# Gated linear attention with a tanh-shrink feed-forward: the state update's products moved behind the output products, into the same PSUM bank

## The chip, the cores and the metric

The kernel runs on one core of one Trainium2 chip. A time is the device time of one execution in microseconds (us). The kernel before was run five times; its time is the median of those. One further execution was recorded by the hardware profiler, and all views below come from it. The engines are named as in the profile: PE is TensorE (matmul), PEld its weight load, DVE is VectorE, ACT is ScalarE, POOL is GpSimd, SP is SyncE, which here only issues transfers.

## The reference

For each of 4 batches and 8 heads, a 48x48 state is decayed and updated at each of 768 positions, and read by q. The result, as rows of 384 features, goes through a feed-forward with h - tanh(h) in the middle.

```python
def _attn_ref(q, k, v, alpha):
    for t in range(S):
        state = alpha[:, :, t, :, None] * state + np.einsum('bhd,bhe->bhde', k[:, :, t], v[:, :, t])
        y[:, :, t] = np.einsum('bhd,bhde->bhe', q[:, :, t], state)

def _moe_ref(x, w_in, w_out):      # x: 3072 x 384, w_in: 384 x 2048, w_out: 2048 x 384
    h = x @ w_in
    return (h - np.tanh(h)) @ w_out
```

## The kernel before

**Units and chunks.** The 3072 rows are worked in 12 units of 256 positions of one batch, three units to a batch. A unit has two chunks of 128 positions. In each chunk the recurrence is written as matrix products: cumulative products of alpha (two scans on VectorE per unit) scale k and q, and then, per chunk:

- `scores` (L757): k times q, 8 matmuls into two PSUM banks, sc0 and sc1.
- `masked` (L767): VectorE multiplies the scores by a triangular mask into SBUF.
- `products` (L780 to L809), task name `y`: the old state times q (L795) and v times the masked scores (L807), 16 matmuls into two PSUM banks. They reuse the banks of the scores. Head pairs g = 0 and 2 go to the first bank, g = 1 and 3 to the second, each to 128 columns, so that half of each bank's 512 columns stays free.
- `features` (L811), task name `x`: ScalarE copies y to SBUF as xT, one copy for each bank (L820).
- `back` (L822): k is transposed on TensorE (L825), into the first bank. `natural` (L827): ScalarE copies it to SBUF as kn (L829).
- `update` (L831): k times v, 8 matmuls (L836), into a tile that takes the second bank anew.
- `state` (L839): VectorE adds it to the decayed state (L844). ScalarE does it for a batch's first chunk (L842).

The last chunk of a batch has no back, natural, update and state. That leaves 20 updates. Unit 0 (`direct` in the code) takes other banks and has its own rules; 18 updates belong to units 1 to 11. An fp32 matmul shows as two MATMUL records in the trace, so an update is x16 there.

**Shapes on the array.** L944, L989, L1004 and L825 use 128 output columns. L807 and L836 use all 128 rows of the array but 48 or 64 columns, in two halves side by side; L795 uses 64 x 64 parts, L757 64 rows by 128 columns.

**The feed-forward.** Each unit has 8 steps. `first` (L944) multiplies xT by two column blocks of w_in. ScalarE and VectorE turn h into g (Square L953, quadratic L957, L961, L965) and for units from 2 on also into sums e (L977 to L979). `second` multiplies g, or the sums, by w_out: L989 for units 0 and 1, L1004 after that.

**The weights.** w_in and w_out arrive as 64-bit numbers in 8 pieces each, called in0 to in7 and out0 to out7 below. A piece is fetched (L43, by SP), read twice by ScalarE (L83, L84) and finished by VectorE (L86, L87). Steps 0 to 7 of unit 0 use them as they come. From unit 2 on, five precombined copies of w_out (`combine`) are needed.

**The order.** A planner (`Planner`, L319) gets every task with an engine, an assumed duration, a rank and the tasks it follows. It plays them through in eight rounds and writes out one fixed order for each engine. The engines then run their queues in order, with waits on semaphores that the framework adds. An assumed duration costs nothing in itself, but changes the order of every engine. In the order before, `update` must follow `x`:

```python
                    go_c("natural", "ACT", 0.6, 6.5, ["back", past and not past_last and f"update {past}"], natural)
                    go_c("update", "PE", 0.5, 9.5, ["natural", f"load v {u}", u > 0 and "x"], update)
```

At the end, a verdict on the ranges of the data (`judge` on VectorE, `gather` on TensorE, L1097) decides whether a general version has to run; here it doesn't.

Of the kernel before, what the change touches and what calls it, by code (L numbers as in the profile page):

```python
# [17 lines left out]
P = 128  # L18
HP = 64
CU = 2  # L20
# [298 lines left out]
class Planner:  # L319
# [13 lines left out]
    def add(self, name, engine, us, rank, after, do, lat=0.25):  # L333
        kind = name.rsplit(" ", 1)[0]
        self.tasks.append((name, engine, us, rank, [a for a in after if a], do, lat, self.last.get(kind)))
        self.last[kind] = name
# [85 lines left out]
def fast(tc, q, k, v, alpha, moe_w_in, moe_w_out, out, w_in, w_out, ident, ok, pad_rows):  # L422
    nc = tc.nc
    B, H, S, D = q.shape
    NP = H // 2
# [10 lines left out]
    V, A, T, GP = nc.vector, nc.scalar, nc.tensor, nc.gpsimd  # L436
# [3 lines left out]
    with ExitStack() as ctx:  # L440
# [84 lines left out]
        ROWS = HP + D  # L525

        def head(g, r):

            return 2 * g + (r + g) % 2
# [17 lines left out]
        for n, (what, s) in enumerate(pieces):  # L549
            rank = RANK[what] + 2 * s  # L550
            held = pieces[n - 4] if n >= 4 else None
# [38 lines left out]
        def gla(u, rank):  # L590
# [5 lines left out]
            m = {}  # L596

            direct = u == 0
# [112 lines left out]
            def done(by, what):  # L711

                return lambda u: [f"{by}{ab} {u}" for ab in "ab"] if by_matmul(u, what) else [f"{by} {u}"]
            kU, qW = done("kU", 1), done("qW", 2)
# [12 lines left out]
            def bank(n, c):  # L727


                if u < PLAIN:  # L730
                    return ps_o.tile([P, NP, P], FP32, name="y", tag=f"o{n if c is None else 2 + n}")
                return ps_sc.tile([P, NP, P], FP32, name="y", tag=f"sc{n}")

            def chunk(c):
                n = i * CU + c
                last = n == NCH - 1
                old, new = states[n % 2], states[(n + 1) % 2]
                me = f"{u}.{c}"
                past = f"{u}.{c - 1}" if c else f"{u - 1}.{CU - 1}" if u else None
                past_last = n == 0  # L740

                def go_c(name, engine, us, k, after, do, **kw):
                    add(f"{name} {me}", engine, us, rank + 6 * c + k,
                        [a if a[-1] in "0123456789" else f"{a} {me}" for a in after if a], do, **kw)
# [35 lines left out]
                def products():  # L780
# [23 lines left out]
                    for g, r, hh in pairs:  # L804
# [3 lines left out]
                                 rhs=m["pm", c][r][:, g, :],  # L808
                                 start=(n == 0 and g < (1 if direct else 2)), stop=True, skip_group_check=True)  # L809

                def features():  # L811
                    to = slice(c * P, (c + 1) * P)
                    y = m["y", c]
                    if n == 0 and direct:
                        A.copy(xT[u][:, 0:KT, to], y[0][:, 0:KT, :])
                        return
                    for x in range(2):
                        of = range(x, KT if direct else NP, 2)
                        rows = P if direct else ROWS
                        A.copy(xT[u][0:rows, of.start:of[-1] + 1:2, to], y[x][0:rows, 0:len(of), :])  # L820
# [8 lines left out]
                    A.copy(kn[:, :, 0:ROWS], m["tp", c][:, :, 0:ROWS])  # L829

                def update():  # L831
                    up = m["up", c] = bank(1, c)
                    for g in range(NP):
                        for r in range(2):
                            size = D if r else HP
                            T.matmul(up[HP * r:HP * r + size, g, 0:D], lhsT=m["kn", c][:, g, HP * r:HP * r + size],  # L836
                                     rhs=vts[u][:, c, head(g, r), :], start=(g == 0), stop=True, skip_group_check=True)

                def state():  # L839
                    up = m["up", c][0:ROWS, :, 0:D]  # L840
                    if n == 0:
                        A.copy(new[0:ROWS, :, 0:D], up)  # L842
                    else:
                        V.tensor_add(new[0:ROWS, :, 0:D], old[0:ROWS, :, 0:D], up)  # L844

                held = []
                if past and not (u == 0 and c == 1):
                    held = [f"masked {past}"]
                    if u > PLAIN or u == PLAIN and c:
                        held += [f"x {past}", not past_last and f"state {past}", not last and "natural"]  # L850
                go_c("scores", "PE", 1.05, 7, kU(u) + qW(u) + held, scores)
                go_c("masked", "DVE", 1.4, 8, ["scores", f"y 0.0" if u == 1 and c == 0 else past and u > 0 and f"y {past}"], masked)
                if n > 0:
                    go_c("decay", "DVE", 0.4, 6, [f"ends {u}", f"state {past}"], decay)
                if direct:
                    go_c("gaps", "ACT", 0.7, 7, [f"load v {u}", n > 0 and "decay", n > 1 and f"y {past}"], gaps)
                go_c("y", "PE", (1.9 if n == 0 else 3.4) if direct else 0.95 if n == 0 else 1.45, 9,
                     ["masked", f"load v {u}", n > 0 and "decay", direct and "gaps",
                      u > 0 and f"x {past}", u > 0 and not past_last and f"state {past}", u > 0 and not last and "natural"], products)
                go_c("x", "ACT", 0.6 if direct and n == 0 else 0.75, 10, ["y"], features)  # L860
                if not last:
                    go_c("back", "PE", 0.5, 6, kU(u) + [past and not past_last and f"state {past}", u > 0 and c and f"x {past}",
                                                       u > PLAIN and f"x {past}", u == PLAIN and not c and f"masked {past}"], back)
                    go_c("natural", "ACT", 0.6, 6.5, ["back", past and not past_last and f"update {past}"], natural)
                    go_c("update", "PE", 0.5, 9.5, ["natural", f"load v {u}", u > 0 and "x"], update)
                    go_c("state", "DVE" if n else "ACT", 0.4, 10,
                         ["update", n > 0 and "decay",
                          n > 0 and not past_last and f"y {past}"], state)

            for c in range(CU):  # L870
                chunk(c)
# [300 lines left out]
```

## Time and profile before

| | |
|---|---|
| median of 5 runs | 601.17 us (601.00 to 602.72) |
| profiled execution | 605.04 us |
| its span, first to last instruction | 603.3 us |
| TensorE's mean granted clock | 0.993 |
| update L836, TensorE | x320 records, 208 / 222 / 257 ns (min / median / max) |
| state L844, VectorE | x16, 354 ns median |
| xT L820, ScalarE | x46, 373 ns median |

Duration columns count a matmul from its start to its modelled end, and such records overlap. What a group takes from TensorE is therefore read from the start of its first matmul to the start of the next group's. A line of the timeline is: start in us, length in us, engine, line of the code, operation, output and inputs, sizes, number of records; in brackets the idle time of the engine ahead of it and what ended that.

### The profile page before, as it was taken

To read this page: it belongs to the slowest core of one execution; us is meant where nothing else is said; L and a number is where in the kernel's file an instruction comes from. 1 tells how busy PE (TensorE), PEld (TensorE's weight loads), DVE (VectorE), ACT (ScalarE), POOL (GpSimd) and SP (SyncE) were. 2 spreads that over 40 slices of the span, in tenths; PEclk is the share of its full clock that TensorE was granted. 3 is DMA by queue.
4 is the path that set the end of the run, shared out by engine and by line. 5 is a ranking of instruction groups with operands and counts; after the bars stand their busy time and mean duration, and the time that the engine had idled before them with its cause. 6 is when DMAs were issued, how large, how long until landed. Compare 5 with 4: busy or idle time off the path is not lost.

```text
span 603.3 us, 10673 instructions
## 1 busy us (share of the span) xinstructions
PE 587.0 (97%) x4113; PEld 508.8 (84%) x4113; DVE 437.6 (73%) x830; ACT 325.6 (54%) x585; POOL 4.0 (1%) x18
## 2 busy tenths in 40 slices
PE   8988999999999999999999999999999999999994
PEld 8766777768998898998898898898898898899994
DVE  7874897988796887986776796885797555634642
ACT  2677896636577575776566264364443333423430
POOL 2000000000000000000000000000000000000000
PEclk9998999999999999999999999999999999999998
DMA  9999962133675544562260131220010000000001
GB/s 182 188 225 228 269 140 59 54 85 79 110 144 123 120 133 116 121 153 75 79 170 27 36 77 28 56 81 3 29 32 1 30 4 1 27 9 1 26 1 33
DMA packets 60188, 50.63 MB, mean 84 GB/s; under 512 B 35264, under 2 KB 49888, under 8 KB 60128
## 3 DMA queue, kind: packets, MB, share of 16 engines
q1 hardware_dynamic: 57216, 48.88, 35.1%
q10 hardware_dynamic: 2912, 0.98, 0.8%
q8 instruction: 34, 0.56, 0.4%
q14 instruction: 26, 0.21, 0.1%
HBM read 44.04 MB, written 4.72 MB: 81 GB/s over the span
## 4 chain that ended last, share of the span: by engine, by line
PE 89%; DMA 7%; SPq 1%; ACT 1%; ACTq 0%; issue 0%; DVE 0%; DVEq 0%
PE h L944 41%; PE o L1004 31%; PE o L989 6%; PE sc L757 4%; PE y L807 4%; DMA raw<-in_moe_w_in_dram 2%; PE y L795 2%; DMA raw<-in_moe_w_out_dram 2%; PE y L836 2%; DMA vt<-in_v_dram 2%; PE y L825 1%; DMA rough<-in_q_dram 1%; SPq L43 1%; DMA ar<-in_alpha_dram 1%; ACTq L581 0%
## 5 line engine op out<-in xcount | busy, mean ns | idle before, releaser
L944 PE MATMUL h<-xT,w_in 128*128 128x256 f32 x1152 | 268.7, 383 | 1.3 <-DVE w_in L87 1.3
L944 PEld LDWEIGHTS h<-xT,w_in 128*128 128x128 f32 x1152 | 215.2, 191 | 31.6 <-DVE w_in L87 1.9
L953 ACT ACTIVATE u<-h 128x512 f32<-128x512 f32 x96 | 57.1, 595 | 181.3 <-PE h L944 180.7
L961 DVE TENSOR_TENSOR w<-h,u 128x512 f32<-128x512 f32 x96 | 65.9, 686 | 91.5 <-ACT u L953 91.4
L1004 PE MATMUL o<-b,e 128*128 128x192 f32 x480 | 91.1, 326 | 0.0
L1004 PE MATMUL o<-w_out,e 128*128 128x192 f32 x320 | 81.2, 335 | 0.0
L1004 PEld LDWEIGHTS o<-b,e 128*128 128x128 f32 x480 | 80.2, 190 | 0.0
L965 DVE SCALAR_TENSOR_TENSOR g<-z,w 128x512 f32<-128x512 f32 x96 | 65.5, 683 | 5.2 <-ACT z L957 2.1
L1004 PE MATMUL o<-b,g 128*128 128x192 f32 x320 | 65.1, 326 | 0.0
L957 ACT ACTIVATE z<-u 128x512 f32<-128x512 f32 x96 | 60.4, 629 | 2.6
L1004 PEld LDWEIGHTS o<-w_out,e 128*128 128x128 f32 x320 | 56.1, 190 | 6.6 <-issue 1.7
L1004 PEld LDWEIGHTS o<-b,g 128*128 128x128 f32 x320 | 54.2, 190 | 0.0
L971 ACT ACTIVATE big<-u 128x1024 f32<-128x1024 f32 x48 | 50.3, 1048 | 0.0
L989 PE MATMUL o<-w_out,g 128*128 128x384 f32 x128 | 44.3, 490 | 0.6 <-DVE w_out L87 0.6
L767 DVE TENSOR_TENSOR pm<-sc,mask 128x512 f32<-128x512 f32 x46 | 29.5, 683 | 12.7 <-PE sc L757 12.7
L989 PEld LDWEIGHTS o<-w_out,g 128*128 128x128 f32 x128 | 23.7, 190 | 14.7 <-DVE w_out L87 0.8
L977 DVE TENSOR_TENSOR e<-g 128x256 f32<-128x256 f32 x80 | 33.3, 416 | 1.4
L978 DVE TENSOR_TENSOR e<-g 128x256 f32<-128x256 f32 x80 | 33.3, 416 | 0.0
L757 PEld LDWEIGHTS sc<-qT,kT 48*128 48x128 f32 x368 | 22.3, 187 | 8.0 <-issue 5.4
L684 DVE TENSOR_TENSOR_SCAN U<-aT,after 128x1032 f32<-128x1032 f32 x12 | 27.6, 2296 | 0.1
L700 DVE TENSOR_TENSOR_SCAN W<-aT,before 128x1032 f32<-128x1032 f32 x12 | 27.6, 2299 | 0.0
L757 PE MATMUL sc<-qT,kT 48*128 48x128 f32 x368 | 26.7, 285 | 0.2 <-DVE rough L469 0.2
(105 smaller groups left out, 533.2 us busy)
## 6 DMA issues: line engine op xcount, KB each, us to landing
raw<-in_moe_w_out_dram SPq DMA_DIRECT2D x16, 768.0 KB, 6.4
raw<-in_moe_w_in_dram SPq DMA_DIRECT2D x32, 288.0 KB, 5.6
vt<-in_v_dram SPq DMA_DIRECT2D x23, 192.0 KB, 3.5
ar<-in_alpha_dram SPq DMA_DIRECT2D x44, 96.0 KB, 2.4
kr<-in_k_dram SPq DMA_DIRECT2D x40, 96.0 KB, 2.3
qr<-in_q_dram SPq DMA_DIRECT2D x40, 96.0 KB, 2.2
raw<-in_moe_w_in_dram SPq DMA_DIRECT2D x32, 96.0 KB, 6.1
out_dram<-same SPq DMA_DIRECT2D x20, 96.0 KB, 1.8
```

The costliest lines, as they stand in the source:

```text
L757: T.matmul(sc[r][:, g, :], lhsT=m["kT"][q, g, c, :], rhs=m["qT"][q, g, c, :], start=True, stop=True)
L767: V.tensor_mul(pm[hh], m["sc", c][hh], mask.unsqueeze(1).to_broadcast([P, NP, P]))
L944: T.matmul(h[:, a, :], lhsT=w_in[:, j, f * P:(f + 1) * P], rhs=xT[u][:, j, :], start=(j == 0), stop=(j == KT - 1))
L953: A.activation(m["u", s], m["h", s], AF.Square, scale=W_SCALE ** -1.5)
L957: A.activation(m["z", s], m["u", s], AF.Square, bias=QB, scale=QA * W_SCALE)
L961: V.tensor_mul(m["w", s], m["h", s], m["u", s])
L965: V.scalar_tensor_tensor(out=g.rearrange("p a c t -> p (a c t)"), in0=m["z", s], scalar=QK, in1=m["w", s], op0=ALU.add, op1=ALU.mult)
L971: A.activation(big, m["us", s // 2].rearrange("p s t -> p (s t)"), AF.Relu, bias=-U_FAST, scale=W_SCALE, accum_out=over[:, n:n + 1])
L977: V.tensor_add(e[:, 0:2, :], g[:, 0], g[:, 1])
L978: V.tensor_sub(e[:, 2:4, :], g[:, :, 1, :], g[:, :, 0, :])
L989: T.matmul(m["o"][c], lhsT=g[:, a, c, :], rhs=w_out[:, f, :], start=(f == 0), stop=(f == FT - 1))
L1004: T.matmul(o[n][:, i], lhsT=g_, rhs=w_, start=(s == 0 and (n, i) in ((0, 0), (1, 0), (2, 1), (3, 0))), stop=(s == FS - 1), skip_group_chec ...
```

## The change

The products of k and v are no longer a task of their own for units 1 to 11. `products` calls `update` at its end, so that its 8 matmuls follow those of y. They write to columns 256 to 447 of y's second bank, which y leaves free, instead of a tile of their own. `state` follows `y` instead of `update`, and reads those columns. `natural` of the next chunk waits for y of the chunk before. Unit 0 keeps its separate update. Three assumed durations in the planner change: scores 1.05 to 1.2; y 0.95 or 1.45 to 1.15 plus 0.55 where there is an old state and 0.45 where there is an update; unit 0's update 0.5 to 0.6.

```diff
@@ products @@
+                    if not direct and not last:
+                        m["up", c] = m["y", c][1].rearrange("p g t -> p (g t)")[:, 2 * P:2 * P + NP * D]
+                        update()
@@ update @@
-                    up = m["up", c] = bank(1, c)
+                    if direct:
+                        m["up", c] = bank(1, c).rearrange("p g t -> p (g t)")[:, 0:NP * D]
+                    up = m["up", c].rearrange("p (g d) -> p g d", d=D)
                     for g in range(NP):
                         for r in range(2):
                             size = D if r else HP
-                            T.matmul(up[HP * r:HP * r + size, g, 0:D], lhsT=m["kn", c][:, g, HP * r:HP * r + size],
+                            T.matmul(up[HP * r:HP * r + size, g, :], lhsT=m["kn", c][:, g, HP * r:HP * r + size],
                                      rhs=vts[u][:, c, head(g, r), :], start=(g == 0), stop=True, skip_group_check=True)
@@ state @@
-                    up = m["up", c][0:ROWS, :, 0:D]
+                    up = m["up", c][0:ROWS].rearrange("p (g d) -> p g d", d=D)
@@ the planner's tasks @@
-                go_c("scores", "PE", 1.05, 7, kU(u) + qW(u) + held, scores)
+                go_c("scores", "PE", 1.2, 7, kU(u) + qW(u) + held, scores)
...
-                go_c("y", "PE", (1.9 if n == 0 else 3.4) if direct else 0.95 if n == 0 else 1.45, 9,
+                go_c("y", "PE", (1.9 if n == 0 else 3.4) if direct else 1.15 + 0.55 * (n > 0) + 0.45 * (not last), 9,
...
-                    go_c("natural", "ACT", 0.6, 6.5, ["back", past and not past_last and f"update {past}"], natural)
-                    go_c("update", "PE", 0.5, 9.5, ["natural", f"load v {u}", u > 0 and "x"], update)
+                    go_c("natural", "ACT", 0.6, 6.5, ["back", past and not past_last and f"{'update' if u == 0 or past == f'0.{CU - 1}' else 'y'} {past}"], natural)
+                    if direct:
+                        go_c("update", "PE", 0.6, 9.5, ["natural", f"load v {u}"], update)
                     go_c("state", "DVE" if n else "ACT", 0.4, 10,
-                         ["update", n > 0 and "decay",
+                         ["update" if direct else "y", n > 0 and "decay",
                           n > 0 and not past_last and f"y {past}"], state)
```

## The prediction

> **What bounds the kernel now.** I read the page first (busy shares, chain that ended last, granted clock), then TensorE's timeline in the steady part, then the timelines of TensorE, ScalarE and VectorE in the first 100 us. The page:
>
> ```profile
> span 603.3 us, 10673 instructions
> PE 587.0 (97%) x4113; PEld 508.8 (84%) x4113; DVE 437.6 (73%) x830; ACT 325.6 (54%) x585; POOL 4.0 (1%) x18
> PEclk9998999999999999999999999999999999999998
> DMA  9999962133675544562260131220010000000001
> PE 89%; DMA 7%; SPq 1%; ACT 1%; ACTq 0%; issue 0%; DVE 0%; DVEq 0%
> ```
>
> TensorE (PE) is busy 97% of the span and makes 89% of the chain; the rest is DMA, at the start. So a nanosecond taken from TensorE after the start is a nanosecond off the end. The steady part, TensorE alone (start us, us, engine, line, tile):
>
> ```profile
> 151.30 0.67 PE L795 MATMUL y<-qT,state 48*64 48x128 f32 x16
> 151.89 1.09 PE L807 MATMUL y<-pm,vt 128*64 128x128 f32 x16
> 152.91 0.59 PE L1004 MATMUL o<-w_out,e 128*128 128x192 f32 x2
> ...
> 155.38 0.67 PE L836 MATMUL y<-vt,kn 128*64 128x48 f32 x16
> 155.98 2.86 PE L944 MATMUL h<-xT,w_in 128*128 128x256 f32 x12
> 158.67 0.49 PE L1004 MATMUL o<-w_out,e 128*128 128x192 f32 x2
> ...
> 160.95 2.75 PE L944 MATMUL h<-xT,w_in 128*128 128x256 f32 x12
> 163.54 0.49 PE L1004 MATMUL o<-w_out,e 128*128 128x192 f32 x2
> ```
>
> Starts, not durations, give the price, since the pipeline overlaps ends. A "first" (L944) from full-array work to full-array work takes 163.54 - 160.95 = 2.59, a "second" (L1004) 160.95 - 158.67 = 2.28. The stretch second, update, first takes 158.67 - 152.91 = 5.76, against 2.28 + 2.59 = 4.87. That is 0.89 more, of which 0.10 is paid by the "second" because it follows y. So **one update standing alone costs 0.79 us**. The single matmul records in the trace divide this: 0.09 until its first matmul starts, 0.60 to the next full-array matmul, 0.10 until that work is back at its pace. The 16 others of units 1 to 11 show 0.79 again, apart from the earliest of them, which also waits.
>
> The start (ScalarE, then TensorE, then ScalarE again):
>
> ```profile
> 24.23 0.54 ACT L820 COPY xT<-y 128x256 f32<-128x256 f32 x2 [0.61 <-PE y L807]
> 29.64 1.09 ACT L83 ACTIVATE more<-raw 128x768 int16<-128x768 uint32 x1 [3.80 <-DMA raw<-in_moe_w_in_dram]
> ```
>
> ```profile
> 54.43 0.67 PE L795 MATMUL y<-qT,state 48*64 48x128 f32 x16 [2.24 <-ACT kn L829]
> 56.23 4.31 PE L944 MATMUL h<-xT,w_in 128*128 128x256 f32 x12
> ```
>
> ```profile
> 66.21 1.09 ACT L83 ACTIVATE more<-raw 128x768 int16<-128x768 uint32 x1 [2.32 <-DMA raw<-in_moe_w_in_dram]
> 69.06 1.06 ACT L83 ACTIVATE more<-raw 128x768 int16<-128x768 uint32 x1
> ```
>
> Until about 72 us the weights arrive at the pace of the DMA engines (the first slices of the DMA row), and the in-order ScalarE stands waiting for them. The 2.24 us pause before 54.43 ends in a stretch at half clock: that "first" takes 4.31 instead of about 2.75.
>
> **The Trainium skill.** "TensorEngine Tiling (Array Packing)", Key Properties: changing the tiling mode, not just the tile, drains TensorE. The trace agrees: the 0.09 and 0.10 appear where a 128-row, 64-column group (L836, L807) meets 128x128 work, and the transposes of L825, full-array too, show no such entry. "PSUM — Partial Sum Buffer", on bank collisions: two engines may not touch one bank in the same partitions at once, disjoint columns included, so PSUM is to be guarded by bank. No run here shows a collision; the new program's waits show the guard (below). "TensorE: Matmul & The Clock Gate", What's actually happening: an idle window of about 3.4 us throttles the array to half clock. The trace has 3.41 us at 0.5 from 55.85, after a pause shorter than such a window.
>
> **The change, part by part.** In the built program's order, TensorE has 18 groups of the update fewer between full-array groups: all 18 of units 1 to 11 now stand directly behind y. The two of unit 0 stay.
> 1. Removed: 18 x 0.79 = 14.3 us of TensorE.
> 2. Added: 18 times the same 16 matmuls in y's mode. No such sequence is in the trace. Within a lone update, the pairs of matmuls start 45 ns (48 weight columns) and 58 ns (64 columns) apart; the entry, the ramp and the drain are y's already. Nearest value: 8 x 0.058 = 0.46. Bounds: 8 x 0.045 = 0.36, and 0.60 if the whole inside of a lone group stays. I take 0.46: 18 x 0.46 = 8.3. Net 0.33 each, **6.0 us for 18**; bounds 18 x 0.43 = 7.7 and 18 x 0.19 = 3.4.
> 3. The wait of update for x (ScalarE's copy of y) goes. It was worth 0.5 us once (at 45.76) and is otherwise covered by "first" and "second" work.
> 4. A new wait: y's second bank now also holds the update's result. ScalarE copies y from it (x) and VectorE adds the update from it (state). In the built program one of the two waits for the other in each of the chunks; in nine, ScalarE's second copy waits for VectorE. Behind it on ScalarE stand a Square and what follows it, and the next "second" waits for those. But ScalarE spent 180.7 us waiting for L944 over 96 steps (1.9 us per step), and the sums needed by the "second" directly behind an update stand ahead of the state in VectorE's order. State itself is 0.35. I take 0; bound +0.5 each, 4.5 in all. The next thing late would be that Square.
> 5. Planner costs: y 2.15 instead of 1.45 with an update of 0.5, scores 1.2 instead of 1.05. They do nothing by themselves, but they re-sort every queue. Sixteen updates lie after the start, with TensorE never idle around them, so 16 x 0.33 = 5.3 is the safe part.
> 6. The start is re-sorted too. On ScalarE the conversion of weight piece in2 now stands ahead of the copy x of unit 0's second chunk (before: behind). in2 lands at 29.6, its two reads take 2.0, so the copy ends near 32.4 instead of 24.8 and the first "first" starts near 32.4 instead of 27.6: 4.7 later. Then the new order runs a "first" ahead of the y of 54.43, which fills that pause. Counting groups from there, TensorE reaches the same work about 3 us before the old kernel at 61 us, and then meets the weights. The new order wants piece out4 one "first" earlier than the old: from there to the end of step 3 of unit 1 lie ten groups of about 2.585 and one transpose group of 0.40, 26.25 us, where the old order has nine and 0.40, 97.76 - 74.10 = 23.66. out4 is read on ScalarE from 69.06 at best, two reads of 1.0, and its VectorE step of 0.96: usable at 72.0, or at 72.95 as before. So the new kernel is at that point at 98.3 to 99.2 instead of 97.76. I take 0.8 later. This swallows the savings of the first two updates (they lie in the DMA-bound stretch) and 0.8 more. Bounds: 2 us gained if out4 comes earlier, and the whole 4.7 plus a throttled window of 1.7 lost. SP's queue moves unit 1's small xT transfers behind the last weight piece; they are needed near 80 us only.
> 7. The tail: the judge's verdict is transposed two "second" steps before the end instead of one. In the old trace the judge ends about 3.6 us after the last "first", and two steps are 4.56, so TensorE doesn't wait. The stores are unchanged: 0.
>
> **Sum.** -5.3 + 0.8 = -4.5. The profiled execution took 605.04 (span 603.3), so 600.5 and a span of 598.8. The profile stands 3.9 above the median of the runs, 601.17; the same difference gives **596.7 us**.
>
> **Rivals.**
> - Savings in full, start no worse, perhaps faster: for it, the new order fills the 2.24 pause. Against it, the weights' pace. -6.0 to -8: 595.2 to 593.2.
> - Only the way back and the entry are saved, since the update keeps its inner 0.60 (its weights may not load ahead behind y). 16 x 0.19 = 3.0, less 0.8: 2.2 faster, 599.0. For it: the inner time holds a ramp between the first two pairs; against it: y's own pairs run evenly behind each other.
> - ScalarE and VectorE wait for each other at the shared bank, and nine Squares are late by 0.5 on TensorE's clock: -4.5 + 4.5 = 0, 601.2. Against: the 1.9 us of room per step.
> - Slower: the late copy of unit 0's features at the start. If its 4.7 is not absorbed by waiting for weights, and one window at half clock (1.7) comes behind the longer pause, the start loses 0.8 + 4.7 + 1.7 = 7.2: -5.3 + 7.2 = +1.9, 603.1. It decides once the start loses over 5.3. For: ScalarE's order is as written; against: the weights that follow come no sooner anyway.
> - That the update isn't merged: excluded by the order on TensorE, for all 18.
>
> **How the numbers follow.** Forecast 0.62 (own range 595.2 to 598.6); full savings 0.13; only entry and way back 0.10; shared bank 0.05; slower 0.10. What a measurement can tell from no change is 0.2%, 1.2 us: faster 0.62 + 0.13 + 0.10 = 0.85, same 0.05, slower 0.10. The range from 593.8 to 600.0 leaves out the slower case, the shared bank and the far end of the full savings.
>
> **What would show it.** In the profile after: the update's group starts within 0.11 of y's last matmul; the block of y and update costs 1.81 + 0.46 = 2.27 in place of 1.81 and 0.79 apart; full-array groups keep 2.59 and 2.28; the "first" of step 3 of unit 1 ends at 98 to 99; ScalarE's copies show waits for VectorE but TensorE none for ScalarE after 75 us; TensorE busy near 582. I am wrong if the block costs 2.4 or more, if TensorE pauses after 100 us, or if the start ends beyond 101.

## The result and the profile after

| | before | after |
|---|---|---|
| median of the runs | 601.46 us (47 runs beside it, 600.31 to 605.58) | 598.68 us (27 runs, 597.57 to 601.57) |
| ratio after to before, 95% interval | | 0.9955 (0.9946 to 0.9963) |
| profiled execution, its span | 605.04, 603.3 us | 598.77, 596.8 us |

The changed kernel is 2.8 us faster. The forecast was 4.5 us faster, 596.7 us, with a range from 593.8 to 600.0. So sign and range held, and the gain is a good third smaller than forecast. First the page of the changed kernel: span, busy time of the engines, granted clock, the DMA row, and the engines' shares of the chain.

```profile
span 596.8 us, 10679 instructions
PE 580.5 (97%) x4111; PEld 509.1 (85%) x4111; DVE 438.0 (73%) x830; ACT 322.8 (54%) x585; POOL 4.0 (1%) x18
PEclk9999999999999999999999999999999999999997
DMA  9999951144675463462430120220100000000001
PE 87%; DMA 8%; SPq 2%; ACT 1%; DVE 1%; issue 1%; ACTq 0%; DVEq 0%
```

TensorE is still the bound. Its busy time fell from 587.0 to 580.5, where about 582 was forecast. The price of the update is read from TensorE's timeline of the changed kernel, in which a y with an update and a y without one stand close together:

```profile
101.65 2.74 PE L996 MATMUL o<-w_out,g 128*128 128x384 f32 x8
104.32 0.67 PE L795 MATMUL y<-qT,state 48*64 48x128 f32 x16
104.92 1.09 PE L807 MATMUL y<-pm,vt 128*64 128x128 f32 x16
105.84 0.62 PE L842 MATMUL y<-vt,kn 128*48 128x48 f32 x16
106.39 2.86 PE L951 MATMUL h<-xT,w_in 128*128 128x256 f32 x12
109.08 2.74 PE L996 MATMUL o<-w_out,g 128*128 128x384 f32 x8
...
115.54 2.74 PE L996 MATMUL o<-w_out,g 128*128 128x384 f32 x8
118.12 2.75 PE L951 MATMUL h<-xT,w_in 128*128 128x256 f32 x12
120.81 0.67 PE L795 MATMUL y<-qT,state 48*64 48x128 f32 x16
121.40 1.09 PE L807 MATMUL y<-pm,vt 128*64 128x128 f32 x16
122.42 2.85 PE L996 MATMUL o<-w_out,g 128*128 128x384 f32 x8
125.11 0.55 PE L829 MATMUL y<-ident,kT 112*128 112x112 f32 x4
```

A `first` (L951) takes 2.59, as before, and a `second` of this kind (L996) 118.12 - 115.54 = 2.58. From 101.65 to 109.08 a `second`, a y with its update, and a `first` take 7.43, so the block costs 7.43 - 5.17 = 2.26. From 118.12 to 125.11 a `first`, a y alone and a `second` take 6.99, so y alone costs 1.82. The update behind y therefore costs 0.44 here, and 0.45 in the mean of the 14 such blocks that can be read. Standing alone it had cost 0.79. In nanoseconds, from the starts of the single records, it is 793 alone and 451 merged, so 0.342 us is saved for each.

The tables below cut every profile at two points of TensorE's timeline. *Start* runs up to the group behind the `first` of step 3 of unit 1 (the forecast's point, 95.19 in the changed kernel). *Middle* runs from there to the start of the last matmul, *tail* from there to the end of the span.

| | start | middle | tail |
|---|---|---|---|
| before, profile shown above | 97.76 | 496.51 | 8.99 |
| before, profile of e1 | 94.30 | 496.51 | 8.79 |
| after, profile shown | 95.19 | 491.82 | 9.78 |
| after, profile of e2 | 94.54 | 491.64 | 9.80 |
| after, profile of e11 | 96.31 | 491.64 | 9.26 |

The middle holds 16 updates and saves 4.7 to 4.9, not the full 16 x 0.342 = 5.47. The start isn't faster, although two further updates lie in it. The tail is 0.3 to 1.0 longer. The experiments ask where these three losses come from.

### The profile page after: what moved, and what is told of

It reads as the page before. It is cut to its first block, busy times and chain, and to the rows that moved or that the text cites. A ratio compares the mean times of both kernels' runs of the same rounds, so it can differ in the third digit from the quotient of the medians.

```text
span 596.8 us, 10679 instructions
## 1 busy us (share of the span) xinstructions
PE 580.5 (97%) x4111; PEld 509.1 (85%) x4111; DVE 438.0 (73%) x830; ACT 322.8 (54%) x585; POOL 4.0 (1%) x18
## 4 chain that ended last, share of the span: by engine, by line
PE 87%; DMA 8%; SPq 2%; ACT 1%; DVE 1%; issue 1%; ACTq 0%; DVEq 0%
PE h L951 40%; PE o L1011 31%; PE o L996 5%; DMA raw<-in_moe_w_in_dram 4%; PE sc L757 3%; PE y L807 3%; DMA raw<-in_moe_w_out_dram 2%; DMA rough<-in_k_dram 2%; PE y L795 2%; PE y L842 1%; SPq L43 1%; PE y L829 1%; ACT more L83 0%; ACT more L84 0%; DMA xT<-xT 0%
## 5 line engine op out<-in xcount | busy, mean ns | idle before, releaser
L951 PE MATMUL h<-xT,w_in 128*128 128x256 f32 x1152 | 266.3, 381 | 2.3 <-ACT xT L824 1.3
L951 PEld LDWEIGHTS h<-xT,w_in 128*128 128x128 f32 x1152 | 214.8, 190 | 32.2 <-DVE w_in L87 1.7
L968 DVE TENSOR_TENSOR w<-h,u 128x512 f32<-128x512 f32 x96 | 65.9, 686 | 88.5 <-ACT u L960 88.1
L996 PE MATMUL o<-w_out,g 128*128 128x384 f32 x128 | 44.3, 489 | 1.2 <-DVE g L972 1.0
L996 PEld LDWEIGHTS o<-w_out,g 128*128 128x128 f32 x128 | 23.9, 190 | 15.3 <-DVE g L972 1.4
```

Of the source, the lines that this page charges most:

```text
L951: T.matmul(h[:, a, :], lhsT=w_in[:, j, f * P:(f + 1) * P], rhs=xT[u][:, j, :], start=(j == 0), stop=(j == KT - 1))
L968: V.tensor_mul(m["w", s], m["h", s], m["u", s])
L996: T.matmul(m["o"][c], lhsT=g[:, a, c, :], rhs=w_out[:, f, :], start=(f == 0), stop=(f == FT - 1))
```

## The experiments

The theory: merging saves 0.34 for each of 18 updates, 6.16 in all, and the three new assumed durations, by re-sorting the queues, give about half of it back, in the start, in the middle and in the tail. The rival: the merge itself brings the losses (the shared bank, or the later `natural`), and the durations are harmless.

**e1 and e2: both kernels again.** No edit.

> The kernel before, unchanged, profiled once more. Theory A (the profile shown of before had a slow start that most executions don't have, and the new start is really about 2.8 us worse than the usual old one): span near 599.5, and the first-products of step 3 of unit 1 end 2 to 3 us ahead of 97.76. Theory B (the old start always ends at 97.8, and the steady part loses something in the new kernel that its profile doesn't show): span near 599.5 too, but the 2 us less are found after 100 us. Ratio 1.000 in both.

> The changed kernel, unchanged, profiled once more. Theory A: its start ends at 95 to 96 again, the merged block costs 2.26, no pause of TensorE after 100 us, ratio 0.9955. Theory B: a pause or a longer block after 100 us.

Medians 601.89 (ratio 1.0012, 0.9993 to 1.0031) and 597.96 (0.9939, 0.9926 to 0.9953). The profile of e1 shows that the profile of before on which the forecast was built had an unusual start. It was 3.5 us longer than that of e1, with the middle the same to the hundredth. TensorE's timeline of e1, from where the old profile had its pause:

```profile
52.57 0.67 PE L795 MATMUL y<-qT,state 48*64 48x128 f32 x16
53.17 1.09 PE L807 MATMUL y<-pm,vt 128*64 128x128 f32 x16
54.19 2.86 PE L944 MATMUL h<-xT,w_in 128*128 128x256 f32 x12
56.98 0.67 PE L836 MATMUL y<-vt,kn 128*64 128x48 f32 x16
```

The 2.24 us pause ahead of y is gone, and so is the `first` of 4.31 us at half clock behind it; this one takes 2.86. Neither shows in e9 either, whose order is the same up to the end: of three profiles of this order, one has them.

**e3: the same order, but the update separate again.** `products` no longer calls `update`; it is issued behind the next full-array group on TensorE. Bank, waits for the bank and durations are those of the changed kernel.

```diff
                     if not direct and not last:
                         m["up", c] = m["y", c][1].rearrange("p g t -> p (g t)")[:, 2 * P:2 * P + NP * D]
-                        update()
+                        pending.append(update)
@@ state, and at the end of first and second @@
+                    flush()
```

> The changed kernel with the 18 merged updates moved behind the next group of first or second products: same bank, same planner, same order of all else. If the array's mode is what counts: each update costs 0.79 again instead of 0.45, so 18 x 0.34 = 6.1 us more than the changed kernel if the start doesn't hide any, about 5.5 with the first two hidden: 604.2 to 604.8, ratio 1.0045 to 1.0055. If the gain came from the new order or from the wait for x that is gone: no more than 1 us above the changed kernel, 599.7, ratio 0.997.

Median 605.76 (1.0067, 1.0053 to 1.0081), 7.8 over e2. The middle is 498.06, 6.42 more than in e2: 16 x 0.342 = 5.47, and one wait of 0.9 that e2 does not have (TensorE's waits of e3 after 100 us; columns: us in total, times, longest):

```profile
PE sc L763 <- ACT kn L839: 0.9, 1, 0.9
PE h L958 <- DMA xT<-xT: 0.2, 1, 0.2
```

The other 1.8 of the 7.8 were not expected. They lie in the start (96.32 against 94.54 in e2), at the upper end of what profiles of the changed kernel show (94.54 to 96.31), and this run doesn't tell what makes them. In the middle, adjacency to y is what saves. With all else of the change in place but that, the kernel is slower than before.

**e4: the durations alone.** The kernel before, with the new numbers in the planner (the update's own share given to `update`).

```diff
-                go_c("scores", "PE", 1.05, 7, kU(u) + qW(u) + held, scores)
+                go_c("scores", "PE", 1.2, 7, kU(u) + qW(u) + held, scores)
...
-                go_c("y", "PE", (1.9 if n == 0 else 3.4) if direct else 0.95 if n == 0 else 1.45, 9,
+                go_c("y", "PE", (1.9 if n == 0 else 3.4) if direct else 1.15 + 0.55 * (n > 0), 9,
...
-                    go_c("update", "PE", 0.5, 9.5, ["natural", f"load v {u}", u > 0 and "x"], update)
+                    go_c("update", "PE", 0.8, 9.5, ["natural", f"load v {u}", u > 0 and "x"], update)
```

> The kernel before with only the planner's new durations (scores 1.2, y 1.15 plus 0.55, update alone 0.8). If the new order is what gives back 2.8 us at the start: 603 to 604.5, ratio 1.003 to 1.005, with the loss ahead of 100 us. If the order is neutral: 601.4, ratio 1.000. If truer durations help the order: 599 to 600.5.

Median 604.84 (601.33 to 607.52; ratio 1.0047, 1.0031 to 1.0063): 2.8 us lost by numbers that compute nothing. Its profiled execution (602.97, below its median) has middle 496.51 and tail 8.67 as before, so what it loses lies in the start: 95.94 against 94.30 in e1 and, in the same order as e1, 95.39 in e9. That is at most 1.6 of the 2.8; the rest isn't in this profile. TensorE's timeline shows what the re-sorted order waits for, a weight piece:

```profile
67.24 2.43 PE L944 MATMUL h<-xT,w_in 128*128 128x256 f32 x10 [2.27 <-DVE w_in L87]
```

The order of e4 isn't that of the changed kernel, so it shows that the start answers to these numbers, not where the changed kernel loses.

**e5 and e9: the verdict's place at the end.** In the changed kernel the transpose of the verdict stands two `second` steps before the end, in the kernel before one. e5 moves it back in the changed kernel. e9 moves it forward in the kernel before, where the judge also moves ahead of the last g on VectorE.

```diff
@@ e5, on the changed kernel @@
-        add("gather", "PE", 0.3, 16 * NU - 20, ["judge"], gather)
+        add("gather", "PE", 0.3, 16 * NU - 20, ["judge", f"second {NU - 1}:{FS - 2}"], gather)
@@ e9, on the kernel before @@
-                    + ([f"second {u}:{s - 1}"] if s else []), second)
+                    + ([f"second {u}:{s - 1}"] if s else []) + (["gather"] if u == NU - 1 and s == FS - 2 else []), second)
```

> The changed kernel with one thing altered: the transpose of the verdict (gather) stands one second step before the end again, as in the kernel before, not two. All other engines keep their order. If the tail's 1.0 us more (last matmul to end of span 9.8 instead of 8.8) comes from the instruction fetch that follows the early branch and meets the last stores: 8.8 again, span and time 1.0 less than the changed kernel, about 597.0, ratio 0.9925. If the tail has another cause (stores, addresses): no change, 598.0, ratio 0.994.

> The kernel before with one thing changed at its end: the transpose of the verdict stands two second steps before the end of TensorE's order, as in the changed kernel, instead of one; VectorE's judge moves ahead of the last g with it. Theory: the earlier verdict makes TensorE fetch the code behind its branch earlier, and this lies beside the last stores. Then the tail (last matmul to end of the span) is 9.7 to 9.9 us instead of 8.7 to 9.0, the issue of the next to last store takes 1.6 to 1.7 us instead of 0.7, and the time is some 1.0 us more than the kernel before, a ratio of 1.0015 to 1.002. Rival, the tail of the changed kernel comes from its re-sorted stores or other things in its order: the tail stays at 8.7 to 9.0 and the time within 0.3 us. Both expect 496.5 from the end of the first of step 3 of unit 1 to the last matmul.

e5: median 597.75 (0.9921, 0.989 to 0.995), tail 8.57 against 9.78 and 9.80. e9: median 602.79 (1.001, 0.9993 to 1.0027), tail 9.53 against 8.79 and 8.99, middle 496.51. SP's timeline has the last two stores as one line; the second number is the time that it took to issue both. In order: the kernel before (e1), the changed kernel (e2), e5, e9.

```profile
592.89 1.05 SPq L1055 DMA_DIRECT2D out_dram<-same  x2
```

```profile
588.27 2.09 SPq L1062 DMA_DIRECT2D out_dram<-same  x2
```

```profile
589.35 0.82 SPq L1062 DMA_DIRECT2D out_dram<-same  x2
```

```profile
593.99 1.75 SPq L1055 DMA_DIRECT2D out_dram<-same  x2
```

Moved early, the verdict makes these issues 0.7 to 1.3 longer; moved late, short again, in either kernel. All 13 profiles of this document divide the same way: where the verdict stands early (five profiles, e3 and e11 among them) the two issues take 1.62 to 2.09 and the tail 9.26 to 9.80, where it stands late (eight) 0.82 to 1.08 and 8.55 to 9.03. The times don't resolve the loss alone: e9 fell short of the 9.7 to 9.9 expected for its tail, and 0.6 us can't be told from nothing in its times; e5 came to 597.75 where about 597.0 was expected, with a start of 95.53. Why an early verdict slows a store is only argued: TensorE comes to its branch sooner, and a 16 KB fetch of instructions, seen among the DMA packets, then starts 2.06 to 2.40 us after the start of the last matmul in the five profiles, just ahead of the issue that becomes long (at 2.46); in the eight others it starts at 3.13 to 4.30, when that issue is over.

**e6: the order of before, merged by hand.** The planner still counts with the old task and the old durations; only what is issued changes. `products`, `update` and `state` have the edits of the change, so that the update stands directly behind y in y's second bank, and the old task issues nothing:

```diff
-                    go_c("update", "PE", 0.5, 9.5, ["natural", f"load v {u}", u > 0 and "x"], update)
+                    go_c("update", "PE", 0.5, 9.5, ["natural", f"load v {u}", u > 0 and "x"], update if direct else lambda: None)
```

> The plan of the kernel before, with its old durations, so every other task keeps its place; only the 18 updates are written out directly behind y, in y's second bank. If the saving is 0.34 per update whatever the plan: the stretch from step 3 of unit 1 to the last matmul takes 496.5 - 5.5 = 491.0, the tail 8.8, the start 94.3 less up to 0.7: time 595.3 to 596.0, ratio 0.990 to 0.991. If the old plan stalls with the longer y, or waits at the shared bank cost time: over 598.

Median 596.44 (594.93 to 600.28; ratio 0.9925, 0.9893 to 0.9956). Middle 491.04, that is 496.51 - 5.47, to the hundredth; tail 8.96. The bank is shared here as well, so neither the bank nor the merge costs anything in the middle. In the start (94.78) y waits 2.0 for kn. The merge didn't make this wait: in the planner y follows `natural` in the kernel before as well, and its first profile had 2.24 at this place. ScalarE copies kn behind a weight piece that arrives late, and here TensorE only comes to it sooner (TensorE, then ScalarE):

```profile
52.69 0.67 PE L795 MATMUL y<-qT,state 48*64 48x128 f32 x16 [2.00 <-ACT kn L833]
```

```profile
50.30 1.06 ACT L83 ACTIVATE more<-raw 128x768 int16<-128x768 uint32 x1 [3.00 <-DMA raw<-in_moe_w_in_dram]
52.13 0.50 ACT L833 COPY kn<-y 128x448 f32<-128x448 f32 x1
```

**e7: unit 0's features ahead of the weight piece.** In the changed kernel, the reads of in2 on ScalarE are made to follow the copy x of unit 0's second chunk, as in the kernel before.

```diff
-            add(f"read {what}{s}", "ACT", 2.1, rank, [f"fetch {what}{s}", older and f"{older[0]}{older[1]}"], a)
+            add(f"read {what}{s}", "ACT", 2.1, rank, [f"fetch {what}{s}", older and f"{older[0]}{older[1]}", (what, s) == ("in", 2) and f"x 0.{CU - 1}"], a)
```

> The changed kernel, with ScalarE's reads of weight piece in2 held behind its copy x of unit 0's second chunk, as in the plan before. If that copy is what makes the start late: the first group of first products starts near 28 instead of 29.7, and step 3 of unit 1 ends at 93 to 94 instead of 94.5; time about 597, ratio 0.992. If the weights' arrival sets the end of the start: 94.5 again, no gain.

Median 599.24 (596.48 to 604.81; ratio 0.9954, 0.9935 to 0.9972), no better than the changed kernel. The first `first` does start at 27.82 instead of 29.84, but the start ends at 95.25, as before the edit: TensorE then waits 1.7 for weight pieces and 2.0 for VectorE's w (L968). This condition, too, made the planner re-sort more than it names: the second `first` moved ahead and the verdict back to its late place. So e7 is not the changed kernel with one thing altered. Its middle got worse, 494.49, from a new wait of 1.75 and a stretch at half clock behind it (TensorE's timeline):

```profile
172.04 1.38 PE L757 MATMUL sc<-qT,kT 48*128 48x128 f32 x16 [1.75 <-ACT kn L833]
173.35 1.01 PE L1011 MATMUL o<-w_out,e 128*128 128x192 f32 x2
174.15 1.49 PE L1011 MATMUL o<-b,g 128*128 128x192 f32 x4
175.43 0.85 PE L1011 MATMUL o<-w_out,e 128*128 128x192 f32 x2
176.07 1.23 PE L1011 MATMUL o<-b,e 128*128 128x192 f32 x6
177.14 2.75 PE L951 MATMUL h<-xT,w_in 128*128 128x256 f32 x12
```

**e8, e10 and e11: the changed kernel with the old durations.** The update is merged as in the change. The planner counts 0.5 for it and 1.45 or 0.95 for the rest of y, 1.05 for scores, as before.

```diff
-                go_c("scores", "PE", 1.2, 7, kU(u) + qW(u) + held, scores)
+                go_c("scores", "PE", 1.05, 7, kU(u) + qW(u) + held, scores)
-                go_c("y", "PE", (1.9 if n == 0 else 3.4) if direct else 1.15 + 0.55 * (n > 0) + 0.45 * (not last), 9,
+                go_c("y", "PE", (1.9 if n == 0 else 3.4) if direct else 0.95 + 0.5 * (n > 0) + 0.5 * (not last), 9,
-                        go_c("update", "PE", 0.6, 9.5, ["natural", f"load v {u}"], update)
+                        go_c("update", "PE", 0.5, 9.5, ["natural", f"load v {u}"], update)
```

> The changed kernel with the planner's old durations (scores 1.05, y 0.95 plus 0.5 with an old state plus 0.5 for the update). The block of y and update costs 2.26 all the same. If the plan matters only by chance at the start: step 3 of unit 1 ends anywhere from 93.5 to 96.5, the rest 491 to 492, time 596 to 600.

> The changed kernel with the old assumed durations, once more, beside the changed kernel on one chip. If its lead is real: 596.4 (595.9 to 596.9), ratio to the kernel before 0.990 to 0.992, 1.5 to 2.5 us under the changed kernel; 491.04 from the end of the first of step 3 of unit 1 to the last matmul, tail 8.5 to 8.6. Rival, its first runs had a start that came out well by chance: 597.5 to 598.3, within 0.7 of the changed kernel.

> The changed kernel again as the partner of the run before: 597.9 to 598.7, ratio to the kernel before 0.994 to 0.9955; tail 9.8, 491.6 to 491.8 from the end of the first of step 3 of unit 1 to the last matmul.

| | median, range | ratio to before, 95% | start | middle | tail |
|---|---|---|---|---|---|
| e8 | 596.36 (594.96 to 596.84, 6 runs) | 0.9903 (0.9875 to 0.9932) | 93.64 | 491.04 | 8.55 |
| e10 | 596.06 (595.66 to 598.97, 6 runs) | 0.9908 (0.9880 to 0.9936) | 94.46 | 491.04 | 8.62 |
| e11, changed kernel beside e10 | 599.16 (596.56 to 600.74, 10 runs) | 0.9943 (0.9922 to 0.9964) | 96.31 | 491.64 | 9.26 |

With the old durations the merge keeps its whole gain, and this version beats both kernels, the changed one by 3.1 us between the medians of e10 and e11 on one chip. Their intervals against the kernel before overlap a little, but five of the six runs of e10 (up to 596.89) lie below nine of the ten of e11 (from 598.86), and e8 had come to the same median. The two profiles divide their difference of 3.09: 1.85 in the start, 0.60 in the middle, 0.64 in the tail. The start's share is the least sure: 93.64 and 94.46 in e8 and e10, 94.54 to 96.31 in three profiles of the changed kernel. The tail's share goes with the verdict, which stands late again in e8 and e10. The middle's 0.60 is one wait. TensorE's timeline of e2, then of e10, at the `first` that opens unit 2:

```profile
127.53 1.16 PE L757 MATMUL sc<-qT,kT 48*128 48x128 f32 x16
128.96 3.12 PE L951 MATMUL h<-xT,w_in 128*128 128x256 f32 x12 [0.27 <-DMA xT<-xT]
131.92 2.42 PE L996 MATMUL o<-w_out,g 128*128 128x384 f32 x7
```

```profile
130.02 1.16 PE L757 MATMUL sc<-qT,kT 48*128 48x128 f32 x16
131.12 2.86 PE L951 MATMUL h<-xT,w_in 128*128 128x256 f32 x12
```

From the scores to this `first` it is 1.43 in e2 and 1.10 in e10. The `first` itself, in e2, takes 2.96 up to the next group where a `first` behind scores takes 2.69 elsewhere: 0.33 and 0.27. What it waits for are the small transfers that put xT into place. SP's timeline of e2, then of e10, says why they are late:

```profile
122.97 0.37 SPq L1045 DMA_DIRECT2D out_dram<-same  x1
123.43 0.38 SPq L1045 DMA_DIRECT2D out_dram<-cross  x1
123.91 1.16 SPq L569 DMA_DIRECT2D vt<-in_v_dram  x2
125.15 3.69 SPq L885 DMA_DIRECT2D xT<-xT  x6
```

```profile
124.84 3.68 SPq L885 DMA_DIRECT2D xT<-xT  x6
128.63 0.53 SPq L1045 DMA_DIRECT2D out_dram<-same  x1
129.26 0.38 SPq L1045 DMA_DIRECT2D out_dram<-cross  x1
```

ScalarE's two copies xT, which the transfers read, in e2, then in e10:

```profile
123.21 0.64 ACT L824 COPY xT<-y 112x256 f32<-112x256 f32 x2
```

```profile
124.17 0.65 ACT L824 COPY xT<-y 112x256 f32<-112x256 f32 x2 [0.41 <-PE y L807]
```

They are done at 123.85 and at 124.82. In the changed order two stores and two loads of v are issued ahead of the six transfers, which start 1.3 after the copies; in e10 they start at once, and the stores and loads follow. In e2 the last of the six is issued at 125.15 + 3.69 = 128.84, just when TensorE is ready, and in e10 at 128.52, 2.6 ahead of it.

## Why the prediction was right, and where its numbers were off

- **Alone 0.79, merged 0.46, 0.33 saved each: right.** 0.79, 0.45 and 0.34. The block of y and update, forecast at 2.27, takes 2.26. The middle of e6, e8 and e10 is shorter by 496.51 - 491.04 = 5.47, which is 16 x 0.342; "5.3" was the safe part. The price was read inside a lone group, from pairs 58 ns apart in the same mode, and this carried over. The rivals with another price for the merged update fall. "TensorEngine Tiling (Array Packing)", Key Properties, in the Trainium skill says that TensorE drains when the tiling mode changes. The runs agree: the same 16 records cost 0.34 less where they need no change of their own (e3 against the changed kernel). That the mode is the reason, and not another effect of the place, was not tested by itself.
- **The shared bank costs nothing: right.** ScalarE waited for VectorE's state in two copies, 1.0 us together in the changed kernel, and TensorE waited for none of it after the start. e6, which shares the bank too, has no loss in its middle.
- **The durations "re-sort every queue" in the middle too: the step that failed.** The forecast named a pause of TensorE after 100 us as a sign of being wrong, and this sign came: 0.39 ahead of one `first` in the shown profile, 0.27 in e2. It had looked at the xT transfers of unit 1 alone. Unit 2's were moved behind stores and loads on SP: 0.60 in e2, 0.78 in the profile shown (491.82 - 491.04).
- **The tail, "The stores are unchanged: 0": failed.** The verdict's move was seen, and only TensorE's wait for the judge was asked about. It cost 0.3 to 1.0 (9.26 to 9.80 against 8.79 and 8.99), through the issue of the stores.
- **The start, 0.8 later: near in size, partly by luck.** Three profiles of the changed kernel end it at 95.35 in the mean; e1 and e9, with the start of the kernel before, at 94.85: 0.5 later, with two updates' savings in it. One kernel's profiles differ by more than that (94.54 to 96.31 for the changed one), so the 0.5 is rough. The forecast's 98.3 to 99.2 was 3 to 4 too late, as it was built on the one long start. There in2 landed at 29.64; in e1 and the changed kernel ScalarE began to read it at 27.56. So the first `first` came 1.8 later than in e1 (29.84 against 28.07), where 4.7 was forecast. The count of ten groups holds: from the `second` that needs out4, at 68.94, to 95.19 it is the forecast 26.25. But out4 wasn't what ended the wait. TensorE's timeline of the changed kernel:

```profile
59.69 2.75 PE L951 MATMUL h<-xT,w_in 128*128 128x256 f32 x12
63.49 2.85 PE L996 MATMUL o<-w_out,g 128*128 128x384 f32 x8 [1.04 <-DVE g L972]
66.17 2.93 PE L951 MATMUL h<-xT,w_in 128*128 128x256 f32 x12
68.94 2.74 PE L996 MATMUL o<-w_out,g 128*128 128x384 f32 x8
```

It was the g of the step before. ScalarE's timeline shows z, from which g is made, in line behind a weight piece:

```profile
59.86 1.08 ACT L83 ACTIVATE more<-raw 128x768 int16<-128x768 uint32 x1 [0.61 <-DVE w_in L87]
60.80 1.04 ACT L84 ACTIVATE more<-raw 128x768 f16<-128x768 f32 x1
61.71 1.12 ACT L964 ACTIVATE z<-u 128x512 f32<-128x512 f32 x2
```

TensorE stood 63.49 - 59.69 - 2.59 = 1.2 for it. That this order comes from the durations is shown (e8, e10); which of the three numbers does it was not tried. The rival that ended slower had the late copy of unit 0's features cost its 4.7 in full; e7, which takes the delay away and whose start gains nothing, fits that it was absorbed, although its order differs elsewhere too. The 0.8 was worked from the arrival of out4, which did not decide; that it came near 0.5 is luck.

- **From profile to median, "the same difference": wrong in its reason.** The 3.9 was taken for something that belongs to a profile. Most of it was that long start. The changed kernel's profile lies 0.1 above its median. The forecast's time came out within 2.0 because the 0.8 was worked against that same start and the difference was then carried over, so that the long start cancelled.

The sum of typical profiles: start +0.5, middle -4.8, tail +0.7, so -3.6 us, where the times say -2.8 (shown), -3.7 (e2) and -3.4 (e11).

## What to carry to other kernels

Here a small group of matmuls in a mode of its own was cheapest directly behind another group of that mode, and its price there could be read from the spacing of its own matmuls. Where a planner writes the order, an assumed duration is part of the change: try the merge with the old numbers too, and read every queue that the new order moves, transfers and the last stores included. Before a forecast is built on the start of one profile, a second profile of the same kernel tells what in it is chance.

## What the runs showed of the hardware that was not expected

Half clock came after pauses shorter than expected. "TensorE: Matmul & The Clock Gate", What's actually happening, in the Trainium skill, gives an idle window of about 3.4 us as what throttles the array. In the shown profile of before the array ran at half clock for 3.41 us from 55.80 (the prediction has 55.85), after a wait of 2.24 and most of y; in e7 for 3.41 us from 172.84, after a wait of 1.75 and most of the scores. Neither pause fills such a window. Nor does the length of the wait decide: 2.00 in e6 and 2.27 in e4 (ahead of 67.24) had no such stretch behind them. What decides stays open. From 172.04 to 177.14 scores and a `second` took 5.10 in e7, where 1.09 and 2.28 are usual: about 1.7 lost.
